# Gated linear attention and a 16-expert layer on one Trainium2 core: a weight load queued ahead of a row fetch, two smaller row limits, and the expert ranking emitted first

## The chip, the cores and the metric

The kernel runs on one core of a Trainium2 chip. The metric is the device time in microseconds of one execution; the time given is the median of three timed runs. A further execution was recorded by the hardware profiler, and all times of single instructions come from that one, counted from the start of its span.

The core has five engines that run their own instruction streams in order and wait for each other by semaphores: TensorE (PE, whose weight loads are listed apart as PEld), VectorE (DVE), ScalarE (ACT), GpSimd (POOL) and SyncE (SP). SP computes nothing here; it issues most DMA transfers. GpSimd issues the indirect ones.

## The reference

```python
# attention: q, k, v, alpha are (4, 8, 768, 48)
for t in range(S):
    state = alpha[:, :, t, :, None] * state + einsum('bhd,bhe->bhde', k[:, :, t], v[:, :, t])
    y[:, :, t] = einsum('bhd,bhde->bhe', q[:, :, t], state)
x = y.transpose(0, 2, 1, 3).reshape(3072, 384)

# experts: 4 groups of 4, w1 (4, 4, 384, 1024), w2 (4, 4, 1024, 384)
g_idx = argmax(x @ w_group, 1);   g_w = softmax(x @ w_group)[g_idx]
for g in range(4):
    xg = x[g_idx == g]
    e_idx = argmax(xg @ w_expert[g], 1);   e_w = softmax(xg @ w_expert[g])[e_idx]
    for e in range(4):
        rows of xg with e_idx == e:
            out[row] = g_w * e_w * (maximum(x[row] @ w1[g, e], 0) @ w2[g, e])
```

Each of the 3072 rows goes to exactly one of 16 experts. With the seed that the reference sets, the experts get 158 to 213 rows each.

## The kernel before

The sequence of every batch is cut into chunks of 128 rows, 24 tiles in all. **Stage one** computes the attention chunk by chunk and routes each tile: scores and outputs on TensorE, decay products on VectorE and GpSimd, states on ScalarE; the rows come out as a tile of `xr`. A small group of tiles is then routed together: VectorE finds the expert and the gate weight (L566 to L603), TensorE counts how many rows each expert has so far, and VectorE works out each row's place (L622 to L632), keeping the running counts in `seen`. GpSimd writes each tile's rows to their places in a table in DRAM, `slots_d`, with one indirect DMA a tile (L635). These scatters are called X0 to X23. Each expert has its own stretch of 3072 places in `slots_d`.

Stage one's instructions are not emitted in program order. Every piece of work is registered with an engine, an assumed duration and what it needs, and a planner (`in_turns`) makes the order of each engine from that. SP's work is registered with `queued`, which puts it in line behind the SP work registered before it, so the order of the calls is the order of SP's queue. All those transfers go through the helper `in_turn` and so carry line L330. The end of that queue is

- the inputs of the last attention units (unit 9 in the buffers that experts' weights use later, unit 10 in buffers of its own),
- `LW`, the weights of expert 0 (`w1` and `w2`, 1.5 MB each), which reuse the input buffers of unit 8,
- `ER`, the early rows: four fetches of the first 128 rows of expert 0 from `slots_d`. They wait for the scatters X0 to X15, after which expert 0 has 128 rows,
- `LX`, the weights of expert 1, two transfers of 1.5 MB each, which reuse the input buffers of unit 9 and so wait for its products.

The early rows are expert 0's first part of 128 rows. They are turned into columns on VectorE (`ET`, L659), go through w1 on TensorE as soon as the last attention tile allows it, and through w2 (L257, 48 matmuls) when all is routed.

**Stage two** is a loop over jobs. Job 0 is the early part, whose matmuls were done in stage one; only its delivery is left. Job 1 is the rest of expert 0 (88 rows), job 2 is expert 1 (188 rows), and jobs 3 to 16 are the other 14 experts in falling order of their row counts, so that fixed row limits fit: the limit of rank r is `cap(r)`. A job's rows are fetched from `slots_d` by SP (`fetch_rows`, L1164, four transfers), turned into columns on VectorE (`columns`, L1043), multiplied with w1 (`hidden_part`, L244), passed through the relu on ScalarE (L247), multiplied with w2 (`result_part`, L257) and copied by ScalarE (L260). One job later they are turned back, weighted and scattered to the output by GpSimd (`deliver_quarters`, L1028 to L1035). Job 1's matmuls come in two halves of 64 columns each, 96 in L244 and 96 in L257; the other jobs have 48 and 48. The weights are double-buffered: job j + 2's are loaded during job j (L228, L230).

The order of the experts is made on the chip by `by_number` (L1114 to L1141, on VectorE): it takes the final counts from `seen`, ranks 14 experts, and gives `order`, which SP reads into a register (L1154) to address rows and weights from job 3 on, and `excess`, the rows beyond each limit. Rows beyond a limit are handled by a loop at the end (behind L1216), which runs once for each 128 of them per expert, and not at all if there are none. Stage two's engines are in program order.

The three places that the change touches in the loop and its limits:

```python
    CAP = 224
    FIXED, EARLY, EARLY_T, BLK = 2, P, (B // 2) * NC + 4, 112
    FIXED_CAPS = [CAP - 8, CAP - 36]
    NS = NE - FIXED
    ...
    jobs = [dict(e=0, n=EARLY, rows=early_rows), dict(e=0, c0=EARLY, n=FIXED_CAPS[0] - EARLY),
            dict(e=1, c0=0, n=FIXED_CAPS[1])]
    jobs += [dict(r=r, c0=0, n=cap(r)) for r in range(NS)]
```

Of the kernel before, what the change touches and what calls it, by code (L numbers as in the profile page):

```python
# [96 lines left out]
def gla_then_hierarchical_moe(  # L97
# [52 lines left out]
# [3 lines that stand above are left out]
    NS = NE - FIXED  # L153

    def cap(r):
        return CAP - 8 - 3 * r - (6 if r >= NS - 2 else 0)

    NX = -(-(N - CAP) // P)
    QW = DM // 4 + 2
# [65 lines left out]
    def load_weights(i, e, start=nc.sync.dma_start):  # L225
        w1 = wp.tile([P, DC, F], F32, name="w1")
        w2 = wp.tile([P, FC, DM], F32, name="w2")
        dma = start(out=w1.rearrange("p c f -> p (c f)"),  # L228
                    in_=w1_d[ds(e, 1)].rearrange("o p f -> p (o f)"))
        start(out=w2.rearrange("p c f -> p (c f)"),  # L230
              in_=w2_d[ds(e, 1)].rearrange("o p f -> p (o f)"))
        weights[i] = (w1, w2)
        return dma.ins
# [45 lines left out]
    with ExitStack() as gla:  # L279
# [58 lines left out]
        def parts(u):  # L338
            return HP // units[u][3]
# [346 lines left out]
        def add(name, engine, takes, serves, emit, needs=(), behind=(), due=NEVER):  # L686


            works[name] = engine, takes, serves, emit, list(needs), list(behind), due
# [6 lines left out]
        def in_line(name, engine):  # L696

            if engine in queue:
                works[name][5].append(queue[engine])
            queue[engine] = name  # L700
# [10 lines left out]
        def each(kind, u):  # L711
            return [f"{kind}{u}.{i}" for i in range(parts(u))]
# [49 lines left out]
        def queued(name, takes, serves, emit, needs=()):  # L762
            add(name, SP, takes, serves, emit, needs)
            in_line(name, SP)
# [35 lines left out]
            {"L": queue_unit, "V": queue_v, "W": queue_rows, "B": queue_fill}[kind](*which)  # L800
        lent = max(u for u in range(NU) if (u + 1) % 3 == 0)
        queued("LW", 7.5, 9.5, lambda: load_weights(0, 0, in_turn), each("KP", lent) + each("QP", lent))
        queued("ER", 2.0, 5.0, read_early, [f"X{EARLY_T - 1}"])
        lent = max(u for u in range(NU) if (u + 1) % 3 == 1)
        queued("LX", 7.5, 9.5, lambda: load_weights(2, 1, in_turn), each("KP", lent) + each("QP", lent))
        add("CONST", POOL, 0.6, 0.7, constants, each("QP", 0))
        add("DESC", DVE, 0.13, 0.25,
             lambda: nc.vector.tensor_copy(out=desc, in_=later["desc_f"]), ["CONST"])
# [179 lines left out]
    def hidden(w1, xt, n, between={}):  # L988
        hT = mp.tile([P, FC, CAP], F32, name="hT")
        for f0 in range(0, FC, 2):  # L990
            for fn in between.get(f0, ()):
                fn()
            hidden_part(bank(), w1, xt, hT, f0, n)()
        return hT

    def result(w2, hT, n):
        yT = results[0]
        results.reverse()
        for d0 in range(0, DC, 2):
            result_part(bank(), w2, hT, yT, d0, n)()  # L1000
        return yT
# [38 lines left out]
    def columns(job):  # L1040
        xt = mp.tile([P, DC, CAP], F32, name="xt_e")
        nb = job["nb"]
        nc.vector.transpose(  # L1043
            out=xt[:, :, 0:32 * nb].rearrange("p c (b t) -> p b c t", t=32),
            in_=job["rows"][:, 0:nb, 0:DM // 4].rearrange("p b (c r) -> p b c r", c=DC))
        return xt

    def destined(job):

        nb, left = job["nb"], job["n"] % 32  # L1050
        dst = mp.tile([P, NB], I32, name="dst_q")
        nc.vector.tensor_copy(out=dst[:, 0:nb], in_=job["rows"][:, 0:nb, QW - 1])  # L1052
        if left:
            none = mp.tile([P, 1], F32, name="none")
            nc.vector.tensor_scalar(out=none, in0=in_tile[:, 0:1], scalar1=float(left),
                                    scalar2=float(4 * N), op0=ALU.is_ge, op1=ALU.mult)
            nc.vector.tensor_tensor(out=dst[:, nb - 1:nb], in0=none,
                                    in1=job["rows"][:, nb - 1, QW - 1:QW], op=ALU.add)
        return dst
# [49 lines left out]
    def by_number():  # L1109

        cnt = rp.tile([P, NE], F32, name="cnt")
        nc.vector.tensor_tensor(out=cnt, in0=seen[:, NT, :], in1=seen[:, 0, :], op=ALU.subtract)  # L1114
        key = rp.tile([P, NS], F32, name="key")
        nc.vector.scalar_tensor_tensor(out=key, in0=cnt[:, FIXED:NE], scalar=float(NE),
                                       in1=tile_f[:, FIXED:NE], op0=ALU.mult, op1=ALU.subtract)
        sq = rp.tile([P, NS, NS], F32, name="sq")
        nc.vector.tensor_tensor(out=sq, in0=key[:, None, :].to_broadcast([P, NS, NS]),
                                in1=key[:, :, None].to_broadcast([P, NS, NS]), op=ALU.is_gt)  # L1120
        rank = rp.tile([P, NS], F32, name="rank")
        nc.vector.tensor_reduce(out=rank, in_=sq, axis=AX.X, op=ALU.add)
        nc.vector.tensor_tensor(out=sq, in0=tile_f[:, 0:NS, None].to_broadcast([P, NS, NS]),
                                in1=rank[:, None, :].to_broadcast([P, NS, NS]), op=ALU.is_equal)
        nc.vector.tensor_tensor(out=sq, in0=sq, in1=tile_f[:, None, FIXED:NE]
                                .to_broadcast([P, NS, NS]), op=ALU.mult)
        order = rp.tile([P, NS], I32, name="order")
        with nc.allow_low_precision("whole numbers below 2**24"):
            nc.vector.tensor_reduce(out=order, in_=sq, axis=AX.X, op=ALU.add)
        excess, ceiling = (rp.tile([P, NE], F32, name=k) for k in ("excess", "ceiling"))  # L1130
        for e, n in enumerate(FIXED_CAPS):
            nc.vector.memset(ceiling[:, e:e + 1], float(n))
        nc.vector.tensor_scalar(out=ceiling[:, FIXED:NE], in0=rank, scalar1=float(cap(1) - cap(0)),
                                scalar2=float(cap(0)), op0=ALU.mult, op1=ALU.add)
        drop = cap(1) - cap(0) + cap(NS - 3) - cap(NS - 2)
        nc.vector.tensor_scalar(out=rank, in0=rank, scalar1=float(NS - 2), scalar2=-float(drop),
                                op0=ALU.is_ge, op1=ALU.mult)
        nc.vector.tensor_tensor(out=ceiling[:, FIXED:NE], in0=ceiling[:, FIXED:NE], in1=rank,
                                op=ALU.add)
        nc.vector.tensor_tensor(out=excess, in0=cnt, in1=ceiling, op=ALU.subtract)  # L1140
        nc.vector.tensor_tensor(out=ceiling, in0=ceiling, in1=seen[:, 0, :], op=ALU.add)  # L1141
        return order, excess, ceiling
# [16 lines left out]
    def fetch_rows(job):  # L1159
        e, nb, c0 = expert(job), job["nb"], job["c0"]  # L1160
        job["rows"] = mp.tile([P, NB, QW], F32, name="xq", bufs=5)
        of = slots_d.rearrange("(e n) w -> e n w", e=NE)[ds(e, 1)]
        for j in range(4):
            dma = nc.sync.dma_start(  # L1164
                out=job["rows"][32 * j:32 * j + 32, 0:nb, :],
                in_=of[:, c0:c0 + 32 * nb, j * QW:(j + 1) * QW].rearrange(
                    "o (b t) w -> (o t) b w", t=32))
        if job is jobs[-1]:
            job["marks"] = mp.tile([P, 2, 2], F32, name="marks", bufs=1)
            nc.sync.dma_start(  # L1170
                out=job["marks"][0:BLK],
                in_=of[:, 0:2 * BLK, QW - 2:QW].rearrange("o (t p) w -> (o p) t w", t=2))
        return dma
# [15 lines left out]

    AHEAD = 2  # L1190
    for j, job in enumerate(jobs):
        for k in range(1 if j == 0 else j + AHEAD, j + AHEAD + 1):
            if k == 3:
                order, excess, ceiling = by_number()
            if k < len(jobs):
                fetch_rows(jobs[k])
        width = job["n"]
        w1, w2 = weights[0] if j < 2 else weights.pop(j)
        dst = destined(job)
        if j == 0:  # L1200
            last = (job, early_xt, dst)
            for t in results:
                nc.gpsimd.memset(t, 0.0)
            xt = columns(jobs[1])
            continue
        hT = hidden(w1, xt, width, {2: [deliver_last]})
        if j + 2 < len(jobs):
            load_weights(j + 2, expert(jobs[j + 2]))
        if j + 1 < len(jobs):
            xt = columns(jobs[j + 1])  # L1210
        if j == 4:
            first, whose, n_more = left_over()
        last = (job, result(w2, hT, width), dst)
# [100 lines left out]
```

## Time and profile before

| | us |
|---|---|
| median of 3 timed runs | 402.22 |
| lowest and highest of them | 398.22, 402.39 |
| the profiled execution | 394.19 |
| its span, from the first to the last instruction | 392.3 |
| TensorE busy in the span | 372.4 |
| mean granted TensorE clock, as a share of full speed | 0.984 |
| DMA: moved in the span | 95.24 MB |

Stage one lasts up to about 123 us of the span, with the early part's last matmuls to 128.3; stage two follows. In the profile a matmul's line is that of the helper that issues it: L244 and L257 are the two expert products, L438 to L537 are attention and routing. In names like `bank<-xt_e,w` the written tile stands ahead of the arrow. A bracket at the end of a timeline row gives how long the engine stood idle before it and what ended that. "SPq" rows are DMA issues on SP's queue: their length is the time to issue, not to land.

### The profile page before, as it was taken

To read this page: it belongs to the slowest core of one execution; us is meant where nothing else is said; L and a number is where in the kernel's file an instruction comes from. 1 tells how busy PE (TensorE), PEld (TensorE's weight loads), DVE (VectorE), ACT (ScalarE), POOL (GpSimd) and SP (SyncE) were. 2 spreads that over 40 slices of the span, in tenths; PEclk is the share of its full clock that TensorE was granted. 3 is DMA by queue.
4 is the path that set the end of the run, shared out by engine and by line. 5 is a ranking of instruction groups with operands and counts; after the bars stand their busy time and mean duration, and the time that the engine had idled before them with its cause. 6 is when DMAs were issued, how large, how long until landed. Compare 5 with 4: busy or idle time off the path is not lost.

```text
span 392.3 us, 9046 instructions
## 1 busy us (share of the span) xinstructions
PE 372.4 (95%) x3462; PEld 355.3 (91%) x3462; DVE 161.5 (41%) x422; ACT 139.3 (36%) x378; POOL 195.6 (50%) x240
## 2 busy tenths in 40 slices
PE   7999999999999699999999999999999999999960
PEld 3888998989989699999999999999999999999950
DVE  6989998999863512137202112021120220220100
ACT  5979999686652121211111121111211211211210
POOL 5988888888655022506244261532614514415430
PEclk9999999999999899999999999999999999999995
DMA  7999999993268497858577586865867868663000
GB/s 267 390 407 416 414 365 367 405 420 126 98 194 322 77 359 213 241 206 261 224 228 209 197 253 232 271 202 200 260 257 239 232 233 299 213 229 130 23 24 10
DMA packets 32700, 95.24 MB, mean 243 GB/s; under 512 B 18470, under 2 KB 18739, under 8 KB 28176
## 3 DMA queue, kind: packets, MB, share of 16 engines
q1 hardware_dynamic: 27552, 85.10, 62.5%
q0 software_dynamic: 5104, 9.55, 7.3%
q8 instruction: 28, 0.46, 0.5%
q14 instruction: 16, 0.13, 0.1%
HBM read 79.47 MB, written 15.57 MB: 242 GB/s over the span
## 4 chain that ended last, share of the span: by engine, by line
PE 83%; DMA 4%; issue 4%; POOL 3%; DVE 2%; SPq 1%; POOLq 0%; ACT 0%; DVEq 0%; ACTq 0%
PE bank L257 31%; PE bank L244 31%; PE zs L438 5%; PE zo L516 5%; DMA w<-in_qka_dram 4%; PE bank L537 4%; PE zo L504 2%; PE bank L456 2%; PE bank L473 2%; SPq L330 1%; POOL out_dram L1035 1%; POOL qp L424 1%; POOL out_dram L1020 1%; PE zs L244 1%; POOL sm L447 0%
## 5 line engine op out<-in xcount | busy, mean ns | idle before, releaser
L1035 POOL DMA_INDIRECT out_dram<-yq,dst_q x99 | 96.2, 972 | 153.1 <-DVE yq L1031 121.1
L244 PE MATMUL bank<-xt_e,w 128*64 128x88 f32 (+15 forms) x816 | 126.5, 323 | 3.1 <-issue 3.1
L244 PEld LDWEIGHTS bank<-xt_e,w 128*128 128x128 f32 (+1 forms) x816 | 124.2, 188 | 3.4 <-issue 3.3
L257 PE MATMUL bank<-hT,w 128*64 128x88 f32 (+15 forms) x816 | 125.2, 318 | 0.0
L257 PEld LDWEIGHTS bank<-hT,w 128*128 128x128 f32 (+1 forms) x816 | 123.0, 184 | 0.0
L1052 DVE CAST dst_q<-xq 128x7 int32<-128x7 f32 (+2 forms) x16 | 2.7, 170 | 168.4 <-DMA out_dram<-yq,dst_q 168.4
L247 ACT ACTIVATE hT<-bank 128x176 f32<-128x176 f32 (+15 forms) x64 | 31.1, 485 | 98.1 <-PE bank L244 98.1
L260 ACT COPY yT<-bank 128x176 f32<-128x176 f32 (+31 forms) x32 | 12.6, 395 | 108.0 <-PE bank L257 108.0
L438 PE MATMUL zs<-qp,kp 48*128 48x128 f32 x384 | 28.2, 285 | 1.3 <-DVE qp L424 1.2
L635 POOL DMA_INDIRECT slots_d<-xr,place x24 | 24.0, 1000 | 8.2 <-issue 3.3
L516 PE MATMUL zo<-sm,v 128*48 128x128 f32 (+1 forms) x384 | 27.1, 279 | 0.4 <-POOL sm L447 0.3
L438 PEld LDWEIGHTS zs<-qp,kp 48*128 48x128 f32 x384 | 23.4, 187 | 3.6 <-DVE qp L424 1.7
L537 PE MATMUL bank<-wr,yt 112*128 112x116 f32 x192 | 26.1, 279 | 0.5 <-ACT sm L868 0.5
L516 PEld LDWEIGHTS zo<-sm,v 128*48 128x48 f32 (+1 forms) x384 | 20.3, 129 | 5.6 <-POOL sm L447 1.8
L537 PEld LDWEIGHTS bank<-wr,yt 112*128 112x128 f32 x192 | 23.3, 192 | 1.0 <-ACT sm L868 0.7
L415 ACT ACTIVATE w<-w,whole 112x128 f32<-112x128 f32 x60 | 19.7, 401 | 1.9 <-DVE whole L406 1.9
L424 POOL TENSOR_TENSOR kp<-w,rev 112x384 f32<-112x384 f32 (+1 forms) x21 | 18.3, 884 | 3.3 <-DVE rev L388 3.3
L424 POOL TENSOR_TENSOR qp<-w,cq 112x384 f32<-112x384 f32 (+1 forms) x20 | 17.0, 858 | 5.4 <-ACT w L415 2.6
L388 DVE TENSOR_TENSOR_SCAN rev<-w,starts 112x387 f32<-112x387 f32 (+1 forms) x22 | 18.4, 868 | 2.9 <-DMA w<-in_qka_dram 2.9
L443 DVE TENSOR_TENSOR sm<-zs,causal 128x512 f32<-128x512 f32 x28 | 18.2, 676 | 2.2 <-PE zs L438 2.1
L398 DVE TENSOR_TENSOR_SCAN cq<-w,starts 112x387 f32<-112x387 f32 (+1 forms) x22 | 19.1, 871 | 0.0
L489 ACT ACTIVATE state<-gained,rev 112x48 f32<-112x48 f32 x64 | 16.2, 326 | 3.2 <-DVE gained L482 2.6
(134 smaller groups left out, 335.3 us busy)
## 6 DMA issues: line engine op xcount, KB each, us to landing
w<-in_w_dram SPq DMA_DIRECT2D x32, 1536.0 KB
w<-in_qka_dram SPq DMA_DIRECT2D x16, 578.0 KB
slots_d<-blank SPq DMA_DIRECT2D x4, 1372.0 KB
qka<-in_qka_dram SPq DMA_DIRECT2D x8, 578.0 KB
v<-in_v_dram SPq DMA_DIRECT2D x3, 1152.0 KB
xq<-slots_d SPq DMA_DIRECT2D x32, 85.8 KB
qka<-in_qka_dram SPq DMA_DIRECT2D x6, 385.5 KB
xq<-slots_d SPq DMA_DIRECT2D x28, 73.5 KB
```

The lines of the kernel that those rows point to most:

```text
L244: nc.tensor.matmul(z[x, k * n:(k + 1) * n], lhsT=w1[:, dc, at + x.start:at + x.stop], rhs=xt[:, dc, 0:n], start=(dc == 0), stop=(dc == DC ...
L247: return lambda: nc.scalar.activation(out=hT[:, f0:f0 + 2, 0:n], in_=z[:, 0:2 * n].rearrange("p (f t) -> p f t", f=2), func=AF.Relu)
L257: nc.tensor.matmul(z[x, i * n:(i + 1) * n], lhsT=w2[:, f, at + x.start:at + x.stop], rhs=hT[:, f, 0:n], start=(f == 0), stop=(f == FC - 1))
L388: nc.vector.tensor_tensor_scan(out=part_of("rev", u, i, A1).rearrange("r c s -> r (c s)")[:, ::-1], data0=a[:, W:0:-1], data1=one_col.to_b ...
L398: nc.vector.tensor_tensor_scan(out=cq, data0=a[:, 0:n * A1], data1=starts[0:R, 0:n * A1], initial=1.0, op0=ALU.mult, op1=ALU.min)
L415: nc.scalar.activation(out=q[:, j, :], in_=q[:, j, :], func=AF.Copy, scale=ready["whole", u][:, i * g + j // k, c:c + 1])
L424: engine.tensor_tensor(out=part_of(kind, u, i, P), in0=of, in1=by[:, :, 1:A1], op=ALU.mult)
L438: nc.tensor.matmul(z[i][:, p, :], lhsT=kp[r, p, c, :], rhs=qp[r, p, c, :], start=True, stop=True)
L516: nc.tensor.matmul(of(z, p)[o], lhsT=vs[b][:, bc, h * D:h * D + o.stop - o.start], rhs=sm[:, i, p, :], start=(p < 2 and bc == 0), stop=Tru ...
L537: nc.tensor.matmul(z[:, at:at + W], lhsT=yt[:, p, :], rhs=wr[:, p, :], start=(p == 0), stop=(p % 2 == 1), skip_group_check=True)
L635: dma = nc.gpsimd.indirect_dma_start(out=slots_by[cs.start + c], out_offset=bass.IndirectOffsetOnAxis(ap=it["to"][:, c:c + 1], axis=0), in ...
L1035: nc.gpsimd.indirect_dma_start(out=out_by.popleft().rearrange("n (j w) -> (n j) w", j=4), out_offset=bass.IndirectOffsetOnAxis(ap=dst[:, b ...
```

## The change

Three edits. The limits `cap(r)` of the last two ranks fall by three rows each, to nine below the line that the other ranks follow instead of six: the last two jobs have 171 and 168 rows instead of 174 and 171. `LX` is registered ahead of `ER`, so SP issues expert 1's two weight transfers ahead of the four early fetches. And `by_number()` is called ahead of the first `fetch_rows`, not between the fetches of job 2 and of job 3.

```diff
     def cap(r):
-        return CAP - 8 - 3 * r - (6 if r >= NS - 2 else 0)
+        return CAP - 8 - 3 * r - (9 if r >= NS - 2 else 0)
...
         queued("LW", 7.5, 9.5, lambda: load_weights(0, 0, in_turn), each("KP", lent) + each("QP", lent))
-        queued("ER", 2.0, 5.0, read_early, [f"X{EARLY_T - 1}"])
         lent = max(u for u in range(NU) if (u + 1) % 3 == 1)
         queued("LX", 7.5, 9.5, lambda: load_weights(2, 1, in_turn), each("KP", lent) + each("QP", lent))
+        queued("ER", 2.0, 5.0, read_early, [f"X{EARLY_T - 1}"])
...
     AHEAD = 2
     for j, job in enumerate(jobs):
+        if j == 0:
+            order, excess, ceiling = by_number()
         for k in range(1 if j == 0 else j + AHEAD, j + AHEAD + 1):
-            if k == 3:
-                order, excess, ceiling = by_number()
             if k < len(jobs):
                 fetch_rows(jobs[k])
```

In the instruction order that results, TensorE, ScalarE and GpSimd keep theirs (ScalarE's last shapes shrink with the rows). On SP the two weight transfers change places with the four early fetches. On VectorE the instructions of `by_number` stand ahead of `dst_q` of the early part (L1052) and `columns` of job 1 (L1043), behind which they stood before.

## The prediction

> **What bounds the kernel now.** I read the page first: shares of busy time, then the chain that ended last.
>
> ```profile
> PE 372.4 (95%) x3462; PEld 355.3 (91%) x3462; DVE 161.5 (41%) x422; ACT 139.3 (36%) x378; POOL 195.6 (50%) x240
> ```
>
> TensorE is busy for 95% of the span, so only two kinds of edit can move the end: less matmul work, or less of the remaining 5% in which TensorE stands. Next I read the chain of work in order of time, to find where it leaves TensorE (start us, us, what):
>
> ```profile
> 122.93 5.37 PE bank L257 x48
> ...
> 128.33 0.49 ACT early_xt L260
> 128.81 2.62 issue
> 131.43 5.09 PE bank L244 x96
> 136.52 3.64 PE bank L257 x96
> ...
> 155.64 8.76 PE bank L244 x48
> 164.40 8.76 PE bank L257 x48
> 173.16 8.64 PE bank L244 x48
> ```
>
> Between the early part's last matmul (end 128.30) and the first matmul of job 1 (131.43) TensorE stands 3.1 us: the one long stop between the first microseconds and the tail. After it, 96 matmuls of L244 take 5.09 us and the 96 of L257, with as many rows, only 3.64. The windows say why (columns: stretch, length, busy time of PE, PEld, DVE, ACT, POOL, granted TensorE clock, DMA share, GB/s):
>
> ```profile
> 114.00:126.00 12.00, 11.88 (x124) 11.13 (x123) 6.63 (x41) 3.26 (x9) 7.67 (x9) 1.00 0.92 362
> 126.00:127.50 1.50, 1.50 (x16) 1.50 (x15) 0.00 (x0) 0.00 (x0) 0.00 (x0) 1.00 0.04 16
> 127.20:130.60 3.40, 1.09 (x10) 0.90 (x9) 0.00 (x0) 0.48 (x1) 0.00 (x0) 1.00 0.25 48
> 130.60:134.00 3.40, 2.57 (x36) 2.60 (x38) 2.87 (x13) 0.32 (x1) 0.00 (x0) 0.50 0.49 92
> 134.00:137.40 3.40, 3.40 (x94) 3.40 (x92) 2.46 (x9) 0.95 (x3) 0.97 (x1) 1.00 0.47 86
> ```
>
> From 130.6 to 134.0 the clock is halved; and the DMA engines are full up to about 125.5, then empty. The timeline shows who is waited for:
>
> ```profile
> 106.00 0.97 POOL L635 DMA_INDIRECT slots_d<-xr,place  x1 [1.82 <-DVE lg L543]
> ...
> 108.90 2.81 SPq L330 DMA_DIRECT2D early_rows<-slots_d  x4
> ...
> 111.82 0.89 SPq L330 DMA_DIRECT2D w<-in_w_dram  x2
> ...
> 122.25 0.97 POOL L635 DMA_INDIRECT slots_d<-xr,place  x1 [1.26 <-ACT blank L247]
> ...
> 127.56 3.67 SPq L1164 DMA_DIRECT2D xq<-slots_d  x8
> 128.33 0.48 ACT L260 COPY early_xt<-bank 128x384 f32<-128x384 f32 x1 [4.98 <-PE bank L257]
> 130.85 0.48 DVE L1043 STREAM_TRANSPOSE xt_e<-xq 128x288 f32<-128x288 f32 x1 [9.29 <-DMA xq<-slots_d]
> 131.25 0.13 DVE L1114 TENSOR_TENSOR cnt<-seen 128x16 f32<-128x16 f32 x1
> ```
>
> X23, the last scatter of rows, starts at 122.25; the fetch of job 1's rows, which waits for it, is issued at 127.56, 5.31 us later. X15 starts at 106.00, and the early rows' fetch that waits for it is issued at 108.90: 2.90 us. The difference is what else is in flight. Expert 1's weights (LX, two transfers of 1.5 MB) stand behind that early fetch on SP's queue, are issued at 111.82 and fill the DMA engines exactly while X16 to X23 go out. SP's own waits show how long the queue was held:
>
> ```profile
> SPq L330 <- DMA slots_d<-xr,place: 37.1, 3, 33.0
> SPq L1164 <- DMA slots_d<-xr,place: 14.5, 5, 12.6
> ```
>
> [...] The stop of 1.17 us before 7.06 lowered nothing.
>
> **The change part by part.** All times are on the profiled execution: span 392.3, time 394.19.
>
> LX ahead of ER. Nothing is added; SP issues the two weight transfers ahead of the four early fetches. They wait only for the last GpSimd product of unit 9 (the qp product on w at 85.35, 0.90 long), so they are issued near 86.3 instead of 111.82. The load in front of them drains at about 91 (the DMA share falls to 0.15 in 91:92). 3.15 MB at the 391 GB/s of 60:80 is an estimate of 8.0 us, and some six scatters of 0.2 MB in between add 3: done by about 102. Between 98 and 106 the DMA share is now 0.28, so the room exists. The early fetch stays at 108.90, since X15 holds it; its four issues are moved past nothing but LX, which is then done. The cover has 4 us (102 to 106); if it went, X15 would land up to 2.41 us late. A DMA load beside the recurrence costs TensorE nothing: one tile's step is 4.6 us both at a full DMA share (zo of L516 at 43.38, then 47.97) and at 0.28 (96.43, then 101.02).
>
> X16 to X23 then go out alone. GpSimd's order and X23's start of 122.25 stay. With X15's 2.90 us, job 1's fetch is issued at 125.15 instead of 127.56. From that issue to the start of columns (L1043) is 3.29 us, with DMA empty before it, so 128.44; from there to the first matmul 0.58, so 129.02. What is late next: that matmul also needs the copy of the early result (128.33 to 128.81), so it can't start before about 128.9 whatever the rows do. I take 129.02: gain 131.43 - 129.02 = 2.41 us, bounds 0 (the scatter is slow for another reason) and 2.5 (the copy's floor).
>
> The clock. [...] the 1.17 us stop left it full speed. So L244 of job 1 should take the 3.64 us of its twin: gain 5.09 - 3.64 = 1.45 us. [...]
>
> by_number first. The same 14 VectorE instructions, 131.25 to 134.49 (3.2 us), move ahead of dst_q and columns of job 1, to 121.5 to 124.7, where VectorE stands idle (9.29 us before L1043). They need only the last seen (L622, 120.69). Columns at 128.44 has 3.7 us in hand, so cost 0; without that cover it would be up to 3.2 on the path. It takes the same time out behind columns, and SP's wait of 2.3 us for order (L1154) goes: job 3's rows come about 4 us sooner, but are first used by columns at 147.28, so gain 0. Its four fetches follow the first eight on SP, so they can't delay job 1's.
>
> Nine rows less. cap falls by 3 for the last two ranks: 174 to 171 and 171 to 168, still six blocks of 32, so fetches, deliveries and instructions stay. From 216 to 213 rows a stage of 48 matmuls falls from 8.76 to 8.64, 0.04 us a row. 3 rows x 2 stages x 2 jobs x 0.04 = 0.48 us on the path, with nothing late behind it: tail deliveries come as much sooner.
>
> Sum: 2.41 + 1.45 + 0.48 = 4.34 us, so 394.19 becomes 389.85. The median of the timed runs is 402.22, 8.03 above the profiled execution; nothing shows where that lies, so I subtract the same 4.34: 397.88, call it 397.9 (-1.1%).
>
> **Rivals.** A: the last scatter's landing doesn't get faster, and only the rows count: 402.22 - 0.48 = 401.7. For it: the waits view lumps eight scatters. Against it: DMA is full until 125.5, and 2.90 stands against 5.31 for the same instruction.
> B: the stop closes, but the timed runs of before had no dip [...]: 402.22 - 2.89 = 399.3. [...] Against it: the one execution seen has the dip.
> C: more goes than the profile shows. The timed runs lie 4 to 8 us above the profiled one and spread over 4.2; if part of that is a longer overlap of scatters and weights, [...] 402.22 - 4.34 - 3.4 = 394.5. For it: X23 started 0.78 us after its places were ready (121.47) where X15 needed 0.27. Against: no record of those runs.
> D, slower: the left-over loop runs. It takes 128 rows at a time when an expert has more rows than its cap, at the very end. Price, an estimate: 3.15 MB of weights at 391 GB/s (8.0), 96 matmuls of 128 rows with nothing beside them (2 x 5.4, more at half clock), four gathers and four scatters at 1.3 (10): some 28 us, so 426. It decides from 172 rows in rank 12 or 169 in rank 13. The reference's inputs give 168 and 158, so three rows would have to be routed differently by rounding, plus one.
>
> **How the numbers follow.** A measurement of this kernel can tell about 1% from no change, 4.0 us, and 398.2 is that bound. Forecast 0.52, of which 0.37 is under the bound (it lies only 0.3 below, and the runs spread 4.2); A 0.07, same; B 0.13, of which 0.03 faster; C 0.22, faster; D 0.06, slower, with any cost that I don't see. So faster 0.37 + 0.03 + 0.22 = 0.62, same 0.15 + 0.07 + 0.10 = 0.32, slower 0.06. The range 394.0 to 401.0 holds the forecast, B and most of C, and leaves out A and D.
>
> **What would show it.** Right: LX issued near 86 to 87; SP's release 2.9 us after X23's start; the chain's issue piece of 2.62 down to about 0.2 or less; L244 of job 1 at 3.6 with clock 1.00; L1114 ahead of L1043 near 121.5; last stages shorter by 0.12. Wrong: the fetch still 5 us behind X23; early rows later than 108.9; the clock still 0.50 near 131; instructions in the loop behind L1216.

## The result, and the profile after

The kernel after takes 398.28 us (median of 20 runs, 394.62 to 400.90), the kernel before, timed beside it, 402.34 (median of 20, 398.22 to 406.12). The ratio is 0.9896, 95% interval 0.9866 to 0.9926, a gain of 4.1 us. The prediction was 397.9. Its total came out, but not by the terms of its sum: the profile after doesn't show what two of its three terms promised, and shows a gain that the sum didn't have.

The profiled execution of after took 399.49 us, its span is 397.5. It is thus 5 us longer than the profiled execution of before, although the timed runs are 4 us shorter. As far as the experiments explain it, TensorE behaves in one of two ways, by chip (job 1's matmuls take 7.4 us at full clock on the one kind and 10.8 to 12.8 on the other), and these two profiles show one each. (Each of the four chips below was used in one session alone, so chip and session can't be told apart; on which chip the profile of before was taken is not on record.) So the two spans are not subtracted here; stages are compared.

The page first. TensorE's share is still 95%, with more time for the same number of instructions:

```profile
PE 378.2 (95%) x3462; PEld 358.1 (90%) x3462; DVE 162.9 (41%) x422; ACT 139.6 (35%) x378; POOL 195.3 (49%) x240
```

The waits of SP's queue (total us, times, longest), 37.1 and 14.5 before:

```profile
SPq L1164 <- DMA slots_d<-xr,place: 5.7, 2, 4.5
SPq L330 <- DMA slots_d<-xr,place: 5.6, 2, 4.4
```

They can't be read as the gain: of the kernels below, the load alone still has 22.1 (L330) and 13.3 (L1164) on the first chip, and one with the load behind ER has 5.6 (L330) on the second. Which of several releasers came last decides where a wait is counted.

The timeline shows what was moved:

```profile
87.30 0.33 SPq L330 DMA_DIRECT2D w<-in_w_dram  x1
...
130.64 0.17 DVE L1114 TENSOR_TENSOR cnt<-seen 128x16 f32<-128x16 f32 x1
131.49 0.97 POOL L635 DMA_INDIRECT slots_d<-xr,place  x1 [3.90 <-ACT blank L247]
134.23 7.62 SPq L1164 DMA_DIRECT2D xq<-slots_d  x12
...
138.51 3.37 PE L244 MATMUL bank<-xt_e,w 128*64 128x88 f32 x83 [1.94 <-issue]
```

LX's second transfer is issued at 87.30, ranking starts right behind the last `seen`, and job 1's fetch is issued 2.74 us behind X23 (131.49 to 134.23) instead of 5.31. So far the prediction holds. But X23 itself starts at 131.49 instead of 122.25, and TensorE still stands 1.94 us ahead of job 1. Stage one was slower in this execution: TensorE's clock is at 0.50 from 106.02 to 112.85, and short stops stand ahead of that. The chain in order of time says what came instead:

```profile
130.98 5.61 PE bank L257 x48
...
137.10 1.41 issue
138.51 3.37 PE bank L244 x83
141.88 0.25 issue
...
144.72 1.00 issue
...
149.56 7.84 PE bank L244 x48
```

Inside job 1's matmuls there are stops of 0.25 to 1.00 us for which the profile shows no waited-for event ("issue"). The profile of before has none of them inside job 1. From job 2 on (149.56) the stages are as before. Behind the last matmul, in what is called the tail here, there is a second difference. The output's last scatters in the timeline, before and then (the last one only) after:

```profile
379.82 0.96 POOL L1020 DMA_INDIRECT out_dram<-yo,dst_m  x1 [6.00 <-DVE yo L1019]
381.08 1.65 POOL L1020 DMA_INDIRECT out_dram<-yo,dst_m  x1 [0.30 <-issue]
```

```profile
390.01 0.94 POOL L1020 DMA_INDIRECT out_dram<-yo,dst_m  x1 [0.30 <-issue]
```

From TensorE's end to the end of the span it is 392.28 - 379.21 = 13.07 us before and 397.47 - 388.13 = 9.34 after. The last two scatters of the output carry 112 rows and what is left of the last job: 59 rows before, 56 after. GpSimd's instruction for it takes 1.65 us with 59 rows and 0.94 with 56.

### The profile page after: what moved, and what is told of

The parts are those of the page before. It is cut to its first block, busy times and chain, and to the rows that moved or that the text cites. A ratio compares the mean times of both kernels' runs of the same rounds, so it can differ in the third digit from the quotient of the medians.

```text
span 397.5 us, 9046 instructions
## 1 busy us (share of the span) xinstructions
PE 378.2 (95%) x3462; PEld 358.1 (90%) x3462; DVE 162.9 (41%) x422; ACT 139.6 (35%) x378; POOL 195.3 (49%) x240
## 4 chain that ended last, share of the span: by engine, by line
PE 83%; DMA 4%; issue 4%; POOL 3%; DVE 2%; SPq 1%; ACT 0%; POOLq 0%; ACTq 0%
PE bank L257 31%; PE bank L244 29%; PE zs L438 5%; PE zo L516 5%; PE bank L537 5%; DMA w<-in_qka_dram 4%; PE zo L504 2%; PE bank L473 2%; PE bank L456 2%; SPq L330 1%; POOL out_dram L1035 1%; POOL qp L424 1%; PE zs L244 1%; POOL sm L447 0%; POOL kp L424 0%
## 5 line engine op out<-in xcount | busy, mean ns | idle before, releaser
L244 PE MATMUL bank<-xt_e,w 128*64 128x88 f32 (+15 forms) x816 | 126.0, 318 | 3.3 <-issue 3.3
L244 PEld LDWEIGHTS bank<-xt_e,w 128*128 128x128 f32 (+1 forms) x816 | 123.0, 184 | 4.2 <-issue 4.1
L257 PE MATMUL bank<-hT,w 128*64 128x88 f32 (+15 forms) x816 | 125.2, 318 | 1.0 <-issue 1.0
L257 PEld LDWEIGHTS bank<-hT,w 128*128 128x128 f32 (+1 forms) x816 | 122.9, 184 | 1.2 <-issue 1.2
L1052 DVE CAST dst_q<-xq 128x7 int32<-128x7 f32 (+2 forms) x16 | 2.7, 169 | 165.3 <-DMA out_dram<-yq,dst_q 165.3
L438 PE MATMUL zs<-qp,kp 48*128 48x128 f32 x384 | 29.9, 287 | 0.6 <-issue 0.5
L516 PE MATMUL zo<-sm,v 128*48 128x128 f32 (+1 forms) x384 | 28.1, 286 | 0.3 <-POOL sm L447 0.3
L537 PE MATMUL bank<-wr,yt 112*128 112x116 f32 x192 | 27.0, 285 | 1.0 <-DMA wr<-in_wr_dram 0.9
L438 PEld LDWEIGHTS zs<-qp,kp 48*128 48x128 f32 x384 | 24.4, 187 | 3.9 <-issue 1.6
L537 PEld LDWEIGHTS bank<-wr,yt 112*128 112x128 f32 x192 | 24.1, 197 | 1.5 <-ACT sm L868 1.1
L1028 DVE STREAM_TRANSPOSE yq<-yT 128x672 f32<-128x672 f32 (+2 forms) x15 | 12.2, 811 | 20.2 <-ACT yT L260 20.1
L524 ACT COPY yt<-zo 112x512 f32<-112x512 f32 x24 | 14.1, 586 | 15.1 <-PE zo L516 8.2
```

Source lines behind the costliest of these rows:

```text
L244: nc.tensor.matmul(z[x, k * n:(k + 1) * n], lhsT=w1[:, dc, at + x.start:at + x.stop], rhs=xt[:, dc, 0:n], start=(dc == 0), stop=(dc == DC ...
L257: nc.tensor.matmul(z[x, i * n:(i + 1) * n], lhsT=w2[:, f, at + x.start:at + x.stop], rhs=hT[:, f, 0:n], start=(f == 0), stop=(f == FC - 1))
L438: nc.tensor.matmul(z[i][:, p, :], lhsT=kp[r, p, c, :], rhs=qp[r, p, c, :], start=True, stop=True)
L516: nc.tensor.matmul(of(z, p)[o], lhsT=vs[b][:, bc, h * D:h * D + o.stop - o.start], rhs=sm[:, i, p, :], start=(p < 2 and bc == 0), stop=Tru ...
L537: nc.tensor.matmul(z[:, at:at + W], lhsT=yt[:, p, :], rhs=wr[:, p, :], start=(p == 0), stop=(p % 2 == 1), skip_group_check=True)
```

## The experiments

Four groups of runs were made, each on one chip with the kernel before beside it. The kernel before takes 394.5 us on the first group's chip, 401.85 on the second's, 403.67 on the third's and 394.48 on the fourth's.

### The three edits alone, and the load's contention put back

The kernel before with only LX ahead of ER:

```diff
-        queued("ER", 2.0, 5.0, read_early, [f"X{EARLY_T - 1}"])
         lent = max(u for u in range(NU) if (u + 1) % 3 == 1)
         queued("LX", 7.5, 9.5, lambda: load_weights(2, 1, in_turn), each("KP", lent) + each("QP", lent))
+        queued("ER", 2.0, 5.0, read_early, [f"X{EARLY_T - 1}"])
```

> Only the first edit: expert 1's weights ahead of the early fetch, the ranking and the row limits as before. Theory (the scatters' contention with that load made the stop ahead of job 1): nearly all of the change's gain is here, 3.4 to 3.9 us, ratio 0.990 to 0.992; in the profile the fetch of job 1 is issued 2.7 to 3.0 us after the last scatter's start, the stop is under 2 us, and the ranking again stands behind columns of job 1. Rival (the ranking's 14 VectorE instructions behind columns were part of what was paid): ratio nearer 0.995.

Measured: 390.55 against 394.5, ratio 0.9907 (0.9877 to 0.9937), a gain of 3.7 us. Its chain:

```profile
128.37 0.07 issue
128.44 3.86 PE bank L244 x96
```

The issue piece of 2.62 us is down to 0.07, TensorE's stop from 3.14 us to 0.59, and L244 runs at full speed. X23 starts at 121.81 and job 1's fetch is issued at 124.55, 2.74 us later. On this chip the profile has both of the prediction's first two terms, 2.41 + 1.45 = 3.86 us predicted. Whether the timed runs of before all paid for the clock, the gain's interval of 2.5 to 4.9 us doesn't tell.

The kernel before with only the smaller limits:

```diff
-        return CAP - 8 - 3 * r - (6 if r >= NS - 2 else 0)
+        return CAP - 8 - 3 * r - (9 if r >= NS - 2 else 0)
```

> Only the row limits: 171 and 168 rows in the last two jobs. Theory: 12 row-stages of 0.04 us, 0.48 us, ratio 0.9988, not to be told from 1. Rival (a left-over loop turn, or shorter tail work): 1.02 or more, or 0.995 and less.

Measured: 388.25, ratio 0.9880 (0.9822 to 0.9937), 4.7 us. The interval, 2.5 to 7.0 us, leaves out the 0.48 us of matmuls that were expected. Those 0.48 us are there: from job 2's first matmul to TensorE's end it is 239.12 us before (140.09 to 379.21) and 238.64 here (137.77 to 376.41). The rest is the tail, 13.07 to 9.20 us. The windows of the two tails (stretch, length, busy time of PE, PEld, DVE, ACT, POOL, clock, DMA share, GB/s), before and then this kernel:

```profile
382.00:384.00 2.00, 0.00 (x0) 0.00 (x0) 0.00 (x0) 0.00 (x0) 0.73 (x1) 0.80 0.14 19
384.00:386.00 2.00, 0.00 (x0) 0.00 (x0) 0.00 (x0) 0.00 (x0) 0.00 (x0) 0.50 0.08 14
386.00:388.00 2.00, 0.00 (x0) 0.00 (x0) 0.00 (x0) 0.00 (x0) 0.00 (x0) 0.50 0.04 15
```

```profile
378.00:380.00 2.00, 0.00 (x0) 0.00 (x0) 0.00 (x0) 0.00 (x0) 0.94 (x1) 0.61 0.37 117
```

Before, the DMA share is 0.14, 0.08 and 0.04 at 14 to 19 GB/s for some 5 us. 59 rows of 1,536 bytes at the 14 to 15 GB/s of the last two windows are some 6 us, an estimate. With 56 rows nearly everything of the last two scatters goes within one window, at 0.37 and 117 GB/s. The last record of the output's scatters ends 7.94 us behind the last matmul before and 4.0 here; what follows it takes 5.1 to 5.2 us in both.

The kernel before with only `by_number` ahead of the first fetches (the third edit of the change):

```diff
+        if j == 0:
+            order, excess, ceiling = by_number()
         for k in range(1 if j == 0 else j + AHEAD, j + AHEAD + 1):
-            if k == 3:
-                order, excess, ceiling = by_number()
```

> Only the ranking moved ahead of the first fetches. Theory: it runs while VectorE waits for the rows, so nothing on the path changes, ratio 1.000; in the profile it stands near 121.5 to 124.7 us and columns of job 1 still waits for its rows. Rival: SP's earlier reading of the order and VectorE's freer stretch behind columns are worth something, ratio 0.997; or the ranking delays columns, above 1.002.

Measured: 394.1, ratio 0.9997 (0.9965 to 1.0028). Nothing, as predicted. Its job 1 starts at 131.04, behind a stop of 2.48 us, and its L244 takes 5.51 us: the load is behind ER, and the half clock is there again.

The kernel after, with expert 1's weights loaded a second time behind ER:

```diff
+        def load_again():
+            for t, of in zip(weights[2], (w1_d, w2_d)):
+                in_turn(out=t.rearrange("p c f -> p (c f)"),
+                        in_=of[ds(1, 1)].rearrange("o p f -> p (o f)"))
...
         queued("ER", 2.0, 5.0, read_early, [f"X{EARLY_T - 1}"])
+        queued("LZ", 7.5, 9.5, load_again, each("KP", lent) + each("QP", lent))
```

> The changed kernel, and expert 1's weights are loaded a second time into the same buffers right behind the early fetch, where their only load stood before: 3 MB more to read, the result is the same. Theory (contention of that load with the last eight scatters): the fetch of job 1 again comes 5 us or more after the last scatter, the stop ahead of job 1 is about 3 us again, and the time is back at that of before less 0.5, ratio 0.997 to 1.002. Rival (what mattered was the place of the load in the queue or its semaphores, not its traffic): it stays at the changed kernel's 0.990.

Measured: 390.03, ratio 0.9889 (0.9861 to 0.9917), 4.4 us. The expected 0.997 to 1.002 is missed, since it had no tail in it; the gain is that of the row limits with their tail (4.7) and no more, so the load's 3.7 us are gone. Its chain:

```profile
128.54 1.81 issue
130.34 3.86 PE bank L244 x96
```

With DMA full again beside X16 to X23 (a share of 0.99 from 112 to 124), job 1's fetch is issued 4.57 us behind X23 (121.98 to 126.55), and the issue piece is back at 1.81. The two kernels above with the load behind ER have 4.15 us there (row limits) and 4.62 (by_number). SP has issued the second load by 112.04 (111.16 + 0.88), so what is left of it when X23 starts is its traffic. It is that traffic, not the place of the load on SP's queue, that held job 1's rows. The half clock did not come back with this stop of 2.33 us.

### The kernel after again, and the last scatter's row count by itself

On the second chip, the kernel after, unchanged:

> The changed kernel, beside the kernel before on the same chip as the other variants. Theory: the two gains are separate and add up, 3.7 us from the load's place (e1) and some 4 us from the row limits, of which 0.5 is matmul rows and 3.5 the last output scatter (56 rows instead of 59): ratio 0.978 to 0.982. Rival: they overlap (the first measurement of the change gave 0.9896 in all), and it is 0.988 to 0.991 again.

Measured: 397.27 against 401.85, ratio 0.9864 (0.9824 to 0.9905), 5.5 us with an interval of 3.8 to 7.1. That holds the gain of rows and tail (4.2 to 4.4) and not the 8.1 that the first group's gains would give if they added up: the expectation is missed, and its rival holds.

The kernel before with its last job cut into 91 and 80 rows instead of 112 and 59; no matmul's size changes but those that turn the last rows back:

```diff
-    FIXED, EARLY, EARLY_T, BLK = 2, P, (B // 2) * NC + 4, 112
+    FIXED, EARLY, EARLY_T, BLK = 2, P, (B // 2) * NC + 4, 91
```

> The kernel before with one number changed: the last job's 171 rows are delivered as 91 and 80 instead of 112 and 59. No matmul of the two expert products changes. Theory [...]: the time from the last matmul to the end of the span falls from 13.1 to between 9 and 10 us, ratio 0.990 to 0.992. Rival (fewer rows in the last scatter make it short): 80 rows take longer than 59, and the tail grows, ratio 1.000 to 1.003.

Measured: 397.21, ratio 0.9886 (0.9845 to 0.9926), 4.6 us, without a row less. Its tail is 9.14 us. The scatter of 80 rows on GpSimd:

```profile
391.63 0.94 POOL L1020 DMA_INDIRECT out_dram<-yo,dst_m  x1 [0.30 <-issue]
```

The kernel after with three rows less still, 168 and 165, so that the last scatter has 53:

```diff
-        return CAP - 8 - 3 * r - (9 if r >= NS - 2 else 0)
+        return CAP - 8 - 3 * r - (12 if r >= NS - 2 else 0)
```

> The changed kernel with the last two limits three rows lower still, 168 and 165 rows, so that the last scatter has 53 rows[...]. Theory: 0.48 us less of matmul rows, but the long tail of 13 us is back: 3.2 us slower than the changed kernel of this job. Rival (fewer rows, shorter tail): 0.5 to 1 us faster than the changed kernel.

Measured: 401.09, ratio 0.9975 (0.9952 to 0.9997): 1.0 us, where the kernel after gained 5.5 on the same chip. The tail is back at 13.10 us:

```profile
389.12 1.57 POOL L1020 DMA_INDIRECT out_dram<-yo,dst_m  x1 [0.30 <-issue]
```

So it is not how many rows the last scatter has, but which number: 80, 60 (below) and 56 are fast (0.94, 0.93 and 0.94 us on GpSimd), 59 and 53 slow (1.65 and 1.57). What sets 59 and 53 apart is not shown. That a count is odd doesn't make it slow: 91 and 105 rows took GpSimd 0.98 and 0.97 us in the scatter ahead of the last one.

The kernel before with ten matmuls of ones (128 x 512, bf16) put into the stop ahead of job 1, meant to keep the clock up; what they write is used by nothing:

```diff
             xt = columns(jobs[1])
+            idle = bank()
+            for _ in range(10):
+                nc.tensor.matmul(idle, lhsT=ones, rhs=ones[:, None, :].to_broadcast([P, 4, P]),
+                                 start=True, stop=True)
```

> The kernel before with ten matmuls of ones (bf16, 128 x 512, not used) put into the stop ahead of job 1, behind the copy of the early result, so that TensorE is not idle there; nothing else changes. Theory [...]: the clock stays 1.00 through the stop, and 0.5 to 1.45 us are gained, ratio 0.9964 to 0.9988. Rival (the clock costs nothing in the timed runs, or the ten matmuls delay job 1): 1.000 or above.

Measured: 401.76, ratio 1.0020 (0.9994 to 1.0047): nothing gained. The profile tells why it couldn't be a test of the clock here: X23 starts at 130.97 and job 1's fetch is issued at 133.72, only 2.75 us later, although LX is behind ER in this kernel. X23 runs 8.7 us later here than in the profile of before, while LX is issued at 112.87, only 1 us later. The windows show that the load is over when X23 goes out (DMA share 0.03):

```profile
128.00:131.00 3.00, 2.35 (x22) 2.19 (x21) 1.52 (x10) 1.41 (x5) 0.03 (x1) 1.00 0.03 10
```

There is no contention left to remove. The filler itself ended at 138.94 and held job 1 up: the turning of its rows (L1043) starts at 137.09, and in before job 1 starts 0.58 us behind that, so without the filler it could have started at some 137.7 instead of 138.87, an estimate. The price of the clock alone stays open.

### A third chip, and what the stops inside job 1 are

The kernel after once more, and the kernel before with only LX ahead of ER once more, side by side:

> The changed kernel again, beside the two variants below. On the chip of e1 to e4, where TensorE had no stops inside job 1, the parts summed to 3.7 us (load) and 4.2 (rows with the tail): theory there 0.979 to 0.982. On the chip of e5 to e8 the tail alone gave 0.9886 and the whole change 0.9864. Theory: the load's part is worth its 3.7 us only where the last scatter comes while the load still runs; where TensorE's own stops hold the last scatter back by 5 us or more, it is worth under 1 us, and the change 0.986 to 0.990. Rival: the parts overlap everywhere, and it is 0.988 whatever the chip.

> Only the load ahead of the early fetch, as in e1, beside the changed kernel of this job. Theory: if the trace has stops of TensorE around 104 to 131 us and the last scatter starts after 127 us, the ratio is 0.997 to 1.001 (the load was already done by then); if the last scatter starts near 122 us, it is 0.989 to 0.993 as in e1. Rival: the queue order is worth 0.991 on every chip.

Measured: the kernel after 401.48 against 403.67, ratio 0.9967 (0.9941 to 0.9993), where 0.986 to 0.990 was expected; the load alone 404.7, ratio 0.9986 (0.9953 to 1.0020), as expected for a last scatter this late (X23 starts at 130.57). The load's place, worth 3.7 us on the first chip, is worth nothing that can be measured here. The chain of the load alone:

```profile
136.17 0.98 issue
137.15 3.86 PE bank L244 x96
141.01 2.60 PE bank L257 x68
143.62 0.37 issue
```

Held against the same kernel on the first chip, its early w2 stage (L257 x48) starts 7.6 us later (130.05 against 122.48), a stop of 1.51 us stays ahead of job 1, and job 1 takes 11.3 us instead of 7.4, with five such stops in it. The kernel after has a tail of 8.96 us here, so the last scatter's gain is there, but its job 1 takes 12.8 us and its clock is halved three times (from 108.50, 128.98 and 146.04). That it gains only 1.3 us on this chip isn't explained beyond that; by_number was not moved alone on such a chip, so an effect of it there isn't ruled out.

The kernel after with job 1 in 48 + 48 matmuls of 128 columns instead of 96 + 96 of 64:

```diff
-        return [slice(0, P)] if n >= P else halves
+        return [slice(0, P)]
```

> The changed kernel with job 1's matmuls in full width: 48 + 48 of 128 columns instead of 96 + 96 of 64, the same result with half the instructions. Theory [...]: there the stops inside job 1 go, and L244 and L257 of job 1 take 10 to 10.5 us together against 10.9 to 12.7 (narrow), so 0.5 to 2 us faster than the changed kernel; on the other chip it is 2.5 to 3 us slower[...]. Rival (the stops have another cause): they stay, and it is 3 us slower or more on either chip.

Measured: 402.72 as the median of six runs from 397.29 to 406.22; the ratio, 0.9897 (0.9823 to 0.9971), rests on three of them and doesn't decide between the theory and its rival. The profile is of the longest of the six. Its chain:

```profile
134.84 9.10 PE bank L244 x48
```

The stops inside job 1 are gone. But the clock stood at 0.50 from 136.4 to 156.9 in this execution: job 2's L244, whose first 2.7 us lie in that stretch, took 9.06 us instead of 7.84, so job 1's time can't be held against the narrow form. Where the stops come from is not shown.

### A version past both

The kernel after with limits twelve lower, as in the run with 53 rows, but cut into 105 and 60 rows:

```diff
-    FIXED, EARLY, EARLY_T, BLK = 2, P, (B // 2) * NC + 4, 112
+    FIXED, EARLY, EARLY_T, BLK = 2, P, (B // 2) * NC + 4, 105
...
-        return CAP - 8 - 3 * r - (9 if r >= NS - 2 else 0)
+        return CAP - 8 - 3 * r - (12 if r >= NS - 2 else 0)
```

> The kernel after with limits twelve lower instead of nine (168 and 165 rows) and the last job cut into 105 and 60 rows instead of 112 and 56. Theory (the count of the last scatter decides the tail[...]): tail about 9.1 us from the last matmul to the end of the span, though 53 rows of the same limits took 13.1; and 0.48 us of matmuls less than the kernel after. On a chip where the kernel before takes about 394 us: 3.66 (load) + 3.7 (tail) + 0.96 (rows) = 8.3 us, ratio about 0.979, if the gains add. On a chip where the kernel before takes about 402 us: about 0.985 (load worth nothing). Rival (fewer rows bring the old tail back[...]): tail 13 us, ratio about 0.988 and 0.996.

Measured: 386.42 against 394.48, ratio 0.9816 (0.9779 to 0.9854), 7.3 us with an interval of 5.8 to 8.7 that holds the 8.3 expected; 13 us of tail, the rival, are not there. Its profile has both gains, the chain first and then the last scatter:

```profile
129.61 3.86 PE bank L244 x96
```

```profile
377.15 0.93 POOL L1020 DMA_INDIRECT out_dram<-yo,dst_m  x1 [0.30 <-issue]
```

Job 1 starts 0.6 us behind the early part, the last scatter takes GpSimd 0.93 us, the tail is 9.20. On a chip without the stops the load and the tail add up. The kernel after itself was not run on such a chip; by this run it would gain some 0.5 us less there, which is an estimate.

## Why the prediction was right in its total and wrong in its parts

| term of the sum | predicted | chips where before takes 394.5 | chips where it takes 402 to 404 |
|---|---|---|---|
| LX ahead of ER, with the clock | 2.41 + 1.45 | 3.7 (0.9907) | 0.6, interval -0.8 to 1.9 (0.9986) |
| rows on TensorE | 0.48 | 0.48 (profile) | 0.48 (profile: 238.64 us behind job 1) |
| the tail | 0 | 3.9 (13.07 to 9.20) | 3.7 (13.08 in the load alone, 9.34 after) |
| by_number | 0 | 0.1, interval -1.1 to 1.4 | not run alone |
| sum | 4.34 | 8.1, added up | 4.2 without the load, 4.8 with it |

That 397.9 lies so near to 398.28 is luck: where before takes 402 us and more, as in the timed runs, the load's 3.86 us did not come as far as the experiments show, and 3.7 us of tail, put at 0, came in their place.

**The step that failed in size** is "with nothing late behind it: tail deliveries come as much sooner". The tail was costed at nothing beyond the matmuls, from the rows' count of blocks, which doesn't change. What had to be asked was how long the last scatter takes at each count: with 59 rows the last record of the output's scatters ends 7.94 us behind the last matmul, with 56 it is 4.0. What could have raised the question stood in the profile of before, a GpSimd instruction of 1.65 us beside one of 0.96 for more rows, and a tail of 13 us of which the prediction looked at nothing. The term is 3.7 us instead of 0; with 0.48 of matmuls that is 4.2, against 4.1 measured. (The prediction's "nine rows" are the limits' distance from the line; it rightly counts three rows in each of two jobs.) Splitting 91 + 80 shows it without any change of rows, 53 rows show it from the other side.

**The step that failed in place** is the use of one profiled execution for the runs that are timed. "Nothing shows where that lies" was said of the 8.03 us between the profiled execution and the median; it was not considered that these 8 us could lie just ahead of the stop. They do, as far as the profiles on the slower chips show: in two kernels with LX still behind ER, the one with the stop filled and the one with 91 + 80 rows, X23 starts at 130.97 and 131.38, the early w2 stage beside it, and job 1's fetch is issued 2.74 to 2.75 us later with LX where it was. So the load was out of the way already, and its new place removes nothing: the stop ahead of job 1 is 1.51 us with 91 + 80 rows, LX behind ER, and 1.51 in the load alone on the third chip, LX ahead. No profile of before itself was taken on such a chip; the kernel with the stop filled is before up to that point.

**What was right.** The mechanism of the load, on the first chip: contention with LX held the last scatter, and without it 2.74 us instead of 5.31 (2.90 predicted), job 1 at 128.44 (129.02 predicted); the second load shows that it is the traffic (4.57 us at a DMA share of 0.99). The copy of the early result became the next wait, as said. In the kernel after LX was issued at 82.81 and 87.30 (86 to 87). X15 is released 2.75 us behind its start (2.90 before), but the early rows' fetch is at 111.13 and not at 108.90, since X15 starts 2.4 us later on that chip. `by_number` costs nothing: L1114 follows the last `seen` directly. The left-over loop does not run; the number of instructions is the same 9,046.

**The clock.** L244 of job 1 took 5.09 us in the profile of before and 5.51 in that of by_number alone, behind stops of 3.14 and 2.48 us; 3.86 behind stops of 2.33 (second load), 1.98 (row limits) and 0.59 (load alone). So the price of the half clock was there in two of the executions that had a long stop and absent in two. Held against 3.86 it is 1.23 us in before, not 1.45: the prediction's 3.64 for L257 is a piece of the chain that begins where L244 ended (136.52), while L257's first matmul starts at 136.34.

Which stop is followed by the half clock is not shown. That a shorter stop would leave full speed was the author's estimate, from the one of 1.17 us in before that did; with the stop of 0.59 us in the load alone it stayed (L244 in 3.86 us). In the 3.41 us ahead of the halved stretch TensorE was busy for 1.10 us in before (127.19 to 130.60) and 0.94 in by_number alone; but in stage one of after it was busy for 2.79 (102.61 to 106.02), and half clock followed as well. No threshold comes out of this.

**The rivals.** A (only the rows count, 401.7) had the load right for the slower chips and the rows' price wrong. B and C moved the load's terms up and down by estimates of the author, and lie on both sides of 398.3. D, the loop, did not come. None had the tail in it.

## What to carry to other kernels

Look at the row count of every small DMA at the end of a kernel: 59 rows ended the kernel 4 us later than 56 or 80 did, and 53 as late. The runs don't show what makes a count slow, so where a job is cut in two, try more than one cut: 91 + 80 and 105 + 60 ended it as early as 112 + 56 did (tails of 9.14, 9.20 and 9.34 us). A bulk load that fills the DMA engines (a share of 0.92 in before, 0.99 in the second load) beside a scatter whose landing is waited for lengthened that wait from 2.7 us to between 4.2 and 5.3, so queue it where nothing is waited for. When timed runs are some per cent longer than the profiled one, the missing time has a place, and a stall that the profile shows may not exist in the runs that count.

## What the runs showed of the hardware

The same kernel takes 394.5 us on two chips and 402 to 404 on two others, and the profiles put most of it between 85 and 150 us: the kernel with the load alone spans 14.9 us more on the third chip than on the first, is 2.8 us late when it issues LX (85.02 against 82.24) and 13.8 late when job 2 is past its w1. In that stretch TensorE stops again and again for 0.25 to 1.0 us with no event waited for. Job 1's 192 matmuls of 64 columns take 7.4 us at full clock on the one kind of chip, from their first to the first of job 2, and 10.8 to 12.8 on the other. What differs between the chips, or between the sessions, stays open.

In the traces the changes of the granted clock lie whole multiples of 3.413 us apart: in before the one halved stretch inside the work lasts 3.413 us, and the full clock behind it 249.17, 73 times that; in after it is 6.827 us, twice that, and 279.89, 82 times; in the kernel after on the third chip the halved stretches begin 20.48 and 17.06 us apart, six and five times. The halved stretches seen here last one such length (130.60 to 134.02 in before), two (106.02 to 112.85 in after) or six (136.39 to 156.87 with job 1 in 128 columns). What lowers the clock is not settled by these runs. In the last two TensorE was busy all through the first 3.41 us of the halved stretch (3.42 of 3.42 us from 106.02 to 109.44 in after, L244 without a stop from 134.84 to 143.94 in the other) and the clock stayed at 0.50, so busy time alone does not decide it.
